# A gMLP input weight fetched from DRAM product by product in layer two instead of being held in SBUF

## The chip, the cores and the metric

The kernel runs on one core of a Trainium2 chip. The core has five engines that work side by side and meet at semaphores: PE (TensorE, matmuls), ACT (ScalarE), DVE (VectorE), POOL (GpSimd) and SP (SyncE, which here only issues transfers). Each engine takes its own instructions strictly in the order of the program. Data sits in DRAM, in SBUF (128 partitions) and, for the results of matmuls, in the banks of PSUM. The metric is the device time of one execution in microseconds; before the change the median of three runs is 1395.2 (1394.91 to 1395.57).

## The reference

Two layers, each a linear attention block and then a gMLP, both with a layernorm ahead of them and a residual connection, on 2048 tokens of width 512 in float32, 896 gated features:

```python
def _A_ref(x, wqkv, wo):                    # linear attention, 32 heads of 16
    pq, pk = phi(q), phi(k)
    kv = einsum("bhsd,bhse->bhde", pk, v); z = einsum("bhsd->bhd", pk)
    o = (pq @ kv) / (pq . z + 1e-6)
    return o @ wo
def _B_ref(x, w_in, w_sp, b_sp, w_out):     # gMLP
    z = _gelu(x @ w_in)                     # 2 * 896 features
    z1 = z[..., :Fh]
    z2 = _layernorm(z[..., Fh:], axis=-1)
    g = einsum("ts,bsf->btf", w_sp, z2) + b_sp[None, :, None]
    return (z1 * g) @ w_out
x = A_x
x = x + _A_ref(_layernorm(x), A_wqkv, A_wo)
x = x + _B_ref(_layernorm(x), B_w_in, B_w_sp, B_b_sp, B_w_out)
x = x + _A_ref(_layernorm(x), A_wqkv, A_wo)
x = x + _B_ref(_layernorm(x), B_w_in, B_w_sp, B_b_sp, B_w_out)
```

Both layers use the same weights. The change concerns the first half of `w_in`, 512 x 896, from which `z1` is made.

## The kernel before

**Numbers.** Every float32 operand of a matmul is held as two parts of type float32r: a high part, rounded by ACT (`high`, L100), and a low part, source minus high part, made by DVE (`low`, L103) or by POOL (L109). A product of two such operands is three matmuls (`mm3`, L113): high by high, high by low, low by high. The third is the first to need the low part of the first operand.

**Room.** SBUF is cut into slots: 22 pages of 128 x 512 floats (`pages`), 6 quads of four pages (`quads`), 4 bigs of seven pages (`bigs`); PSUM into 8 banks. `Slots.get` gives the slot that has been free longest, `put` appends it to the free list; whoever first writes a slot waits by semaphore for the last user of its former tile. The order of all instructions on every engine is the order of the Python program.

**Stages of a layer.** `P1` (q, k, v side of the attention), `transition`, `P2` (attention's output, residual, layernorm, both halves of the gMLP's input product), `P4` (spatial product, gate, output product). The change is in `P2`.

**P2's steps.** There are 16 token tiles of 128 rows. Step s of `P2.run` (L684) works on several tiles at once, in this order of the program: loads for the next steps on SP (`loadx`, `qturn.load`); `b_high`, `b_low`: the turned and divided queries of tile s in two parts; `c`: 12 matmuls, attention's output of tile s-1; `c2`, `c_stats`: residual and statistics (DVE, then three small instructions on POOL, `rs` L182 and L183 and `nb` L185); `c3`: store of x on SP, normalisation on ACT (L191), turn; `a` for a later tile (POOL L544); `d_high`, `d_low`: the turned normalised rows of tile s-2 in two parts (from step 6 on through DRAM, `yt`); `e4`: normalisation of an earlier gate row; `e`, `e2`, `e3`: 24 matmuls of 448 columns for the second half of `w_in`, gelu, statistics (POOL again, `rs` and `nb`); then `f` twice.

**The products `f`.** The first half of `w_in` is used turned: product (n, f) takes 128 features f and 512 tokens n, 12 matmuls of 512 columns, gelu on ACT (L677), store to DRAM (L680). There are 7 x 4 = 28 products in a layer, seven for each group of four tiles. The first group is complete in step 5, so the products run from step 6 on, two per step (one in steps 9, 13, 17); step 18 runs two, and the five that are left run at the head of `P4.run` (L1002), so that the last seven stand back to back.

**The weight before.** `w_in1()` (L167) makes a `Weight` of seven pieces of one page. `fetch` loads a piece into a page (SP), `piece` splits it into the parts `h` and `l` in two bigs (ACT L101, POOL L109 where `pool` is true) and gives the page back. The transition fetches two pieces; steps 1 to 7 of `P2.run` split one each, last thing in the step. Each layer does it anew; the bigs are given back at the head of `P4.run`.

**POOL's other work in P2.** In layer one `sums.tick()` (from step 8 on) makes sums of spatial weights on POOL (L772) from pages that SP loads just before; in layer two nothing of that is left.

Of the kernel before, what the change touches and what calls it, by code (L numbers as in the profile page):

```python
# [53 lines left out]
def mixer_kernel(ctx: ExitStack, tc: tile.TileContext, x_in, wqkv, wo_d, win1_d, win2_d, wsp_d, bsp_d, wout_d,  # L54
# [63 lines left out]

    class Weight:


        def __init__(self, slots, shape, pieces, turned=False):
            self.slots, self.shape, self.pieces, self.turned = slots, shape, pieces, turned
            self.h = self.l = None
            self.raw = deque()
            self.n_load = self.n_split = 0
# [6 lines left out]
        def piece(self, pool=False):  # L133
            if self.n_split >= len(self.pieces):
                return False
            if self.h is None:
                self.h = self.slots.get(self.shape, F32R)
                self.l = self.slots.get(self.shape, F32R)
            if not self.raw:
                self.fetch()  # L140
            r = self.raw.popleft()
            n = len(self.shape)
            flat = "p a b -> p (a b)" if n == 3 else "p a b c -> p (a b c)"
            s = slice(self.n_split * 512, (self.n_split + 1) * 512)
            h, l = self.h.rearrange(flat)[:, s], self.l.rearrange(flat)[:, s]
            if self.turned:
                split(feats(h, True), feats(l, True), feats(r, False), pool)
            else:
                split(h, l, r, pool)
            pages.put(r)  # L150
            self.n_split += 1
            return True
# [7 lines left out]

    def w_square(src, off, turned=False):
# [5 lines left out]
    def w_in1():  # L167
        return Weight(bigs, [P, NF, 4, P], [win1_d[f] for f in range(NF)])
# [78 lines left out]
    class P1:  # L247
# [164 lines left out]
        def run(self):  # L412
# [5 lines left out]
            for s in range(1, NT + 2):  # L418
                self.loadx(s + 3)
                self.turn.load(s + 1)  # L420
                turned = 2 <= s < NT and s not in self.turn.by_pe
# [35 lines left out]
    def transition(p1, p2):  # L457
# [21 lines left out]
        p2.win1.fetch()  # L479
        p2.win1.fetch()  # L480
# [44 lines left out]
    class P2:  # L525
        def __init__(self, p1):
            self.L = L = p1.L
            self.p1 = p1
            self.win1, self.win2 = w_in1(), p1.win2
# [135 lines left out]
        def f(self):  # L665
# [4 lines left out]
            w = self.win1  # L670
            b = banks.get(PAGE)
            for c in range(4):
                mm3(b, (w.h[:, f, c, :], w.l[:, f, c, :]), (h[:, c, :], l[:, c, :]), c == 0, c == 3)
# [10 lines left out]
        def run(self, sums):  # L684
            w1 = self.win1
            for s in range(1, NT + 3):
                self.loadx(s + 1)
                self.qturn.load(s + 1)
                if s in self.qturn.by_pe:
# [48 lines left out]
                w1.piece(True)  # L738
                w1.fetch()
# [55 lines left out]
    class P4:  # L795
# [203 lines left out]
        def run(self, nxt):  # L999
# [3 lines left out]
            while p2.f():  # L1003
                pass
            p2.win1.free()
# [100 lines left out]
```

## Time and profile before

| | |
|---|---|
| median of the runs | 1395.2 us |
| the profiled execution's own time | 1395.31 us |
| its span, first instruction to last | 1393.5 us |
| granted TensorE clock | 1.00 |
| matmuls | 6270 |
| DRAM read, written | 156.63 MB, 67.90 MB |
| P2's products in layer one, layer two | from 189.2 us, from 879.3 us |

How to read what follows. Times are in us from the start of the span, unless ns is written. A row of a timeline gives start, duration, engine, line of the kernel, operation, tile written, arrow, tiles read; in brackets the idle time before and who ended it. Tiles are named by their slots: `pg` a page, `qd` a quad, `bg` a big, `bank` a PSUM bank. `SPq` is SP issuing a transfer. A row of groups gives the count, total busy time, mean ns of one, and idle time before. Matmuls of 512 columns are listed with 0.39 us but start every 0.23 us, since they overlap. A row of transfers gives the kilobytes of one and the median us from issue to landing.

### The profile page before, as it was taken

Reading aid. Unit: us, or ns where it says so; the run is one execution under the profiler, and the core shown is the slowest. Engines: PE = TensorE matmul, PEld = TensorE weight load, DVE = VectorE, ACT = ScalarE, POOL = GpSimd, SP = SyncE. Lnnn points to the kernel's source line nnn. Section 1 sums busy time; section 2 is a strip of 40 time slices with the busy share of each in tenths; the row PEclk is TensorE's granted clock in tenths of the full one; section 3 lists DMA queues with packets and bytes.
Section 4 is the critical chain, followed back from the end, with each engine's and each line's share of the span. In section 5 each row is a group of like instructions: output and inputs, shape, how many; then the busy total and the mean of one; then the engine's idle time right before and its main releaser. Section 6 shows DMA issues by size and latency. Waiting matters only on the chain.

```text
span 1393.5 us, 17586 instructions
## 1 busy us (share of the span) xinstructions
PE 1387.4 (100%) x6270; PEld 1164.0 (84%) x6270; DVE 879.5 (63%) x1251; ACT 582.1 (42%) x899; POOL 416.9 (30%) x502
## 2 busy tenths in 40 slices
PE   9999999999999999999999999999999999999998
PEld 7888888888888888888888888888888888888887
DVE  6775777853755587664567767876426445776642
ACT  6674543444432234241366655444333432342410
POOL 3343344543135541431023424432100000223310
PEclk9999999999999999999999999999999999999999
DMA  5542256776679964354645314555334323544542
GB/s 176 168 131 59 90 166 218 259 226 217 215 235 295 298 228 136 121 203 159 211 129 176 111 46 121 174 176 175 104 122 142 101 96 129 168 134 156 169 143 91
DMA packets 142457, 225.70 MB, mean 162 GB/s; under 512 B 11937, under 2 KB 50593, under 8 KB 142369
## 3 DMA queue, kind: packets, MB, share of 16 engines
q1 hardware_dynamic: 142368, 224.57, 50.1%
q8 instruction: 49, 0.80, 0.3%
q14 instruction: 40, 0.32, 0.1%
HBM read 156.63 MB, written 67.90 MB: 161 GB/s over the span
## 4 chain that ended last, share of the span: by engine, by line
PE 98%; DVE 1%; DMA 0%; POOL 0%; ACT 0%; issue 0%; SPq 0%; POOLq 0%; ACTq 0%
PE bank L117 19%; PE bank L116 19%; PE bank L115 19%; PE bank L897 13%; PE bank L898 13%; PE bank L899 13%; PE bank L203 1%; PE bank L390 0%; DMA pg<-in_wsp_dram 0%; POOL pg L772 0%; ACT z_z L191 0%; DVE st L178 0%; ACT qd L101 0%; POOL rs L183 0%; DVE den L557 0%
## 5 line engine op out<-in xcount | busy, mean ns | idle before, releaser
L898 PE MATMUL bank<-qd,pg 128*128 128x512 f32 x800 | 311.4, 389 | 0.0
L897 PE MATMUL bank<-qd,pg 128*128 128x512 f32 x800 | 311.4, 389 | 0.0
L899 PE MATMUL bank<-qd,pg 128*128 128x512 f32 x800 | 311.4, 389 | 0.0
L863 DVE TENSOR_TENSOR qd<-qd,qd 128x1024 fp32r<-128x1024 f32 x112 | 157.9, 1410 | 157.2 <-ACT qd L856 154.2
L856 ACT ACTIVATE qd<-qd 128x1024 fp32r<-128x1024 f32 x112 | 118.6, 1059 | 239.1 <-DMA qd<-s 101.7
L899 PEld LDWEIGHTS bank<-qd,pg 128*128 128x128 f32 x800 | 150.2, 188 | 31.4
L897 PEld LDWEIGHTS bank<-qd,pg 128*128 128x128 f32 x800 | 150.1, 188 | 31.2
L898 PEld LDWEIGHTS bank<-qd,pg 128*128 128x128 f32 x800 | 150.2, 188 | 31.0
L919 POOL TENSOR_TENSOR bg<-bg,pg 128x512 f32<-128x512 f32 x56 | 78.9, 1413 | 320.7 <-DMA pg<-z 308.6
L117 PE MATMUL bank<-qd,pg 128*128 128x512 f32 x384 | 149.9, 390 | 0.0
L182 POOL TENSOR_SCALAR rs<-mv 128x1 f32<-128x1 f32 x96 | 38.0, 396 | 355.4 <-DVE mv L180 351.8
L191 ACT ACTIVATE pg<-pg,nb,rs 128x512 f32<-128x512 f32 x63 | 51.0, 810 | 179.0 <-POOL nb L185 172.8
L772 POOL TENSOR_TENSOR pg<-pg,pg 128x512 f32<-128x512 f32 x64 | 93.9, 1467 | 94.4 <-DMA pg<-in_wsp_dram 88.5
L115 PE MATMUL bank<-qd,pg 128*128 128x512 f32 x288 | 112.3, 390 | 0.0
L116 PE MATMUL bank<-qd,pg 128*128 128x512 f32 x288 | 112.3, 390 | 0.0
L115 PE MATMUL bank<-bg,qd 128*128 128x448 f32 x256 | 94.1, 368 | 0.0
L117 PE MATMUL bank<-bg,qd 128*128 128x448 f32 x256 | 93.6, 366 | 0.1
L116 PE MATMUL bank<-bg,qd 128*128 128x448 f32 x256 | 93.7, 366 | 0.0
L117 PE MATMUL bank<-qd,bg 128*128 128x512 f32 x224 | 87.5, 391 | 0.0
L116 PE MATMUL bank<-qd,bg 128*128 128x512 f32 x224 | 87.5, 390 | 0.0
L115 PE MATMUL bank<-qd,bg 128*128 128x512 f32 x224 | 87.3, 390 | 0.0
L116 PE MATMUL bank<-wo,qd 128*128 128x512 f32 x224 | 87.2, 389 | 0.0
(128 smaller groups left out, 2606.9 us busy)
## 6 DMA issues: line engine op xcount, KB each, us to landing
qd<-s SPq DMA_DIRECT2D x64, 512.0 KB, 3.5
qd<-in_wsp_dram SPq DMA_DIRECT2D x48, 512.0 KB, 4.2
pg<-in_wsp_dram SPq DMA_DIRECT2D x64, 256.0 KB, 5.2
s<-pg SPq DMA_DIRECT2D x64, 256.0 KB, 5.0
pg<-x SPq DMA_DIRECT2D x64, 256.0 KB, 3.1
z<-pg SPq DMA_DIRECT2D x56, 256.0 KB, 2.7
pg<-z SPq DMA_DIRECT2D x56, 256.0 KB, 3.9
x<-pg SPq DMA_DIRECT2D x48, 256.0 KB, 2.6
```

The lines of the kernel that those rows point to most:

```text
L115: nc.tensor.matmul(out, ah, bh, start=start, stop=False)
L116: nc.tensor.matmul(out, ah, bl, start=False, stop=False)
L117: nc.tensor.matmul(out, al, bh, start=False, stop=stop)
L182: nc.gpsimd.tensor_scalar(rs, mv[:, 1:2], LN_EPS, None, op0=OP.add)
L191: nc.scalar.activation(y, x, AF.Identity, bias=nb, scale=rs)
L772: nc.gpsimd.tensor_tensor(t, a, b, op=OP.add)
L856: nc.scalar.activation(w[:, 0], r, AF.Copy)
L863: nc.vector.tensor_sub(w[:, 1], r, w[:, 0].bitcast(F32))
L897: m(out, h[:, o], w[:, 0, j, :], start=start, stop=False, skip_group_check=True)
L898: m(out, h[:, o], w[:, 1, j, :], start=False, stop=False, skip_group_check=True)
L899: m(out, l[:, o], w[:, 0, j, :], start=False, stop=stop, skip_group_check=True)
L919: nc.gpsimd.tensor_tensor(u, u, z1, op=OP.mult)
```

## The change

In layer one each split of a piece of the weight also notes its two parts for storing; at the head of every step of `P1.run` and `P2.run`, `flush` issues up to four of the noted stores on SP. The stores go to 14 DRAM tiles of a page each. In layer two the weight takes no bigs and nothing is split. `Parts` keeps up to three products' parts ahead, each in two pages (high, low) that POOL's transfers fill from those DRAM tiles; product (n, f) takes the next two pages and gives them back as soon as its matmuls are in the program. The parts are fetched anew for each of the four groups, 28 x 2 transfers of 256 KB. `fetch` stands at the end of each step from step 4 on, and behind each product at the head of `P4.run`. The transfer's source is declared float32 and its destination float32r.

```diff
--- before.py
+++ after.py
@@ -116,11 +116,18 @@
         nc.tensor.matmul(out, ah, bl, start=False, stop=False)
         nc.tensor.matmul(out, al, bh, start=False, stop=stop)
 
+    stores = deque()
+
+    def flush(n=4):
+        for _ in range(min(n, len(stores))):
+            d, part = stores.popleft()
+            nc.sync.dma_start(d, part.bitcast(F32))
+
     class Weight:
 
 
-        def __init__(self, slots, shape, pieces, turned=False):
-            self.slots, self.shape, self.pieces, self.turned = slots, shape, pieces, turned
+        def __init__(self, slots, shape, pieces, turned=False, keep=None):
+            self.slots, self.shape, self.pieces, self.turned, self.keep = slots, shape, pieces, turned, keep
             self.h = self.l = None
             self.raw = deque()
             self.n_load = self.n_split = 0
@@ -148,6 +155,8 @@
             else:
                 split(h, l, r, pool)
             pages.put(r)
+            if self.keep is not None:
+                stores.extend(zip(self.keep[self.n_split], (h, l)))
             self.n_split += 1
             return True
 
@@ -158,6 +167,28 @@
         def free(self):
             self.slots.put(self.h, self.l)
 
+    class Parts:
+
+
+        def __init__(self, kept, times, ahead):
+            self.todo = deque(kept * times)
+            self.ahead = ahead
+            self.have = deque()
+
+        def fetch(self):
+            while self.todo and len(self.have) < self.ahead:
+                parts = [pages.get([P, 4, P], F32R) for _ in range(2)]
+                for t, d in zip(parts, self.todo.popleft()):
+                    nc.gpsimd.dma_start(t, d.rearrange("p (c f) -> p c f", c=4))
+                self.have.append(parts)
+
+        def take(self):
+            if not self.have:
+                self.fetch()
+            return self.have.popleft()
+
+    kept_in1 = [[dram.tile(PAGE, F32, name=f"win1_{f}_{i}") for i in range(2)] for f in range(NF)]
+
     def w_square(src, off, turned=False):
         return Weight(quads, [P, 4, 512], [src[c * P:(c + 1) * P, off:off + 512] for c in range(4)], turned)
 
@@ -165,7 +196,7 @@
         return Weight(bigs, [P, 4, 512], [wo_d[c * P:(c + 1) * P, :] for c in range(4)])
 
     def w_in1():
-        return Weight(bigs, [P, NF, 4, P], [win1_d[f] for f in range(NF)])
+        return Weight(bigs, [P, NF, 4, P], [win1_d[f] for f in range(NF)], keep=kept_in1)
 
     def w_in2():
         return Weight(bigs, [P, 4, FH], [win2_d[f] for f in range(NF)])
@@ -418,6 +449,7 @@
             for s in range(1, NT + 2):
                 self.loadx(s + 3)
                 self.turn.load(s + 1)
+                flush()
                 turned = 2 <= s < NT and s not in self.turn.by_pe
                 if turned:
                     self.T_high(s)
@@ -476,8 +508,9 @@
         banks.put(zb)
         p2.a(0)
         p1.late_phi()
-        p2.win1.fetch()
-        p2.win1.fetch()
+        if p2.L == 0:
+            p2.win1.fetch()
+            p2.win1.fetch()
         p2.zeps = small.tile([P, 32], F32, name="zeps", bufs=1)
         nc.vector.tensor_reduce(p2.zeps, p2.zbc.rearrange("p (h d) -> p h d", d=16), axis=mybir.AxisListType.X,
                                 op=OP.add)
@@ -526,7 +559,7 @@
         def __init__(self, p1):
             self.L = L = p1.L
             self.p1 = p1
-            self.win1, self.win2 = w_in1(), p1.win2
+            self.win1, self.win2 = (w_in1() if self.L == 0 else Parts(kept_in1, NCHK, 3)), p1.win2
             self.qturn, self.xturn = Turn(f"qt{L}", range(5), True), Turn(f"yt{L}", range(4))
             self.qp, self.qT, self.x, self.ms, self.xB, self.z, self.zms = {}, {}, {}, {}, {}, {}, {}
             self.fq = deque()
@@ -668,9 +701,15 @@
             n, f = self.fq.popleft()
             h, l = self.xT[n]
             w = self.win1
+            if self.L == 0:
+                wh, wl = w.h[:, f], w.l[:, f]
+            else:
+                wh, wl = w.take()
             b = banks.get(PAGE)
             for c in range(4):
-                mm3(b, (w.h[:, f, c, :], w.l[:, f, c, :]), (h[:, c, :], l[:, c, :]), c == 0, c == 3)
+                mm3(b, (wh[:, c, :], wl[:, c, :]), (h[:, c, :], l[:, c, :]), c == 0, c == 3)
+            if self.L > 0:
+                pages.put(wh, wl)
             if f == NF - 1:
                 quads.put(*self.xT.pop(n))
             t = pages.get(PAGE)
@@ -686,6 +725,7 @@
             for s in range(1, NT + 3):
                 self.loadx(s + 1)
                 self.qturn.load(s + 1)
+                flush()
                 if s in self.qturn.by_pe:
                     self.c(s - 1)
                     self.b_high(s)
@@ -735,8 +775,11 @@
                 self.f()
                 self.fq.extend(self.fnext)
                 self.fnext = []
-                w1.piece(True)
-                w1.fetch()
+                if self.L == 0:
+                    w1.piece(True)
+                    w1.fetch()
+                elif s >= 4:
+                    w1.fetch()
                 if s > 7:
                     sums.tick()
                 if s >= NT + 1:
@@ -1001,8 +1044,10 @@
             self.prepare(0, 0)
             self.fetch(2)
             while p2.f():
-                pass
-            p2.win1.free()
+                if p2.L > 0:
+                    p2.win1.fetch()
+            if p2.L == 0:
+                p2.win1.free()
             self.prepare(1, 1)
             self.fetch(3)
             self.prepare(None, 2)
```

## The prediction

> **What bounds the kernel now.** I read the page first (busy shares, then the chain that ended last), then the windows of the stage in which layer two would use the new transfers, then the timeline of each engine inside it.
>
> ```profile
> span 1393.5 us, 17586 instructions
> PE 1387.4 (100%) x6270; PEld 1164.0 (84%) x6270; DVE 879.5 (63%) x1251; ACT 582.1 (42%) x899; POOL 416.9 (30%) x502
> PE 98%; DVE 1%; DMA 0%; POOL 0%; ACT 0%; issue 0%; SPq 0%; POOLq 0%; ACTq 0%
> ```
>
> TensorE is busy for all but 6 us of the span and is 98% of the chain. The change adds and removes no matmul, so its gain can be no more than a few stalls that are hardly there; the question is whether it makes PE wait. The same stage (from the first gMLP product to the first of the last seven) in layers one and two:
>
> ```profile
> core 0: us, PE busy (x) PEld busy (x) DVE busy (x) ACT busy (x) POOL busy (x), PEclk, DMA share, GB/s
> 189.20:332.70 143.50, 143.44 (x662) 123.82 (x661) 96.25 (x152) 57.75 (x94) 65.82 (x101) 1.00 0.69 222
> 879.30:1022.40 143.10, 143.10 (x662) 124.01 (x662) 88.12 (x152) 58.42 (x94) 39.97 (x81) 1.00 0.49 155
> ```
>
> Layer one carries the spatial sums on POOL besides: 26 us more POOL work and 67 GB/s more traffic cost 0.4 us in 143. So traffic alone is cheap here: the change's 56 loads of 256 KB (14.7 MB) in some 160 us are about 90 GB/s, which takes layer two to about 245 GB/s, just above layer one. What the 0.4 us is shows in the chain of waits, and it is the pattern to fear:
>
> ```profile
> 222.66 5.49 DMA pg<-in_wsp_dram
> 229.68 1.29 POOL pg L772
> 232.03 0.28 POOL nb L185
> 233.70 0.70 DVE qd L104
> 234.44 0.48 PE bank L117
> ```
>
> POOL executes in order. While it waits at L772, the row statistics behind it wait too; ACT normalises late, the split of the turned row (`d_low`) is late, and PE's third matmul of `e` stands still. In layer two POOL will stand in issues of transfers instead.
>
> **Layer one: the 14 stores.** Step s issues on SP the two stores of piece s-1. A store must wait for POOL's subtract, and the whole SP queue waits with it:
>
> ```profile
> 189.92 1.29 POOL L109 TENSOR_TENSOR bg<-pg,bg 128x512 fp32r<-128x512 f32 x1
> ...
> 190.93 0.38 SPq L97 DMA_DIRECT2D pg<-qt  x1
> 194.36 0.38 SPq L227 DMA_DIRECT2D qt<-pg  x1
> ```
>
> Step 6 shows it: the subtract ends at 191.21, SP is done with its loads at 191.31 and has nothing until 194.36. Two issues of 0.38 us end at 192.1. Cost 0, covered by 3.0 us of SP idleness; without that cover it would be 0.8 us of SP per step, not on PE's path.
>
> **Layer two, removed.** Seven loads on SP, seven roundings on ACT (0.6 us each), seven subtracts on POOL. PE waits for none of them, but the subtract stands in POOL's order and slows a small DVE add beside it. Rows of the timelines of POOL, DVE, ACT and PE in order of time (start and duration in us, then the instruction, in brackets how long the engine had been idle and for whom):
>
> ```profile
> 861.86 1.29 POOL L109 TENSOR_TENSOR bg<-pg,bg 128x512 fp32r<-128x512 f32 x1
> 862.37 0.18 DVE L180 BATCH_NORM_AGGREGATE mv<-st 128x2 f32<-128x6 f32 x1
> 863.25 0.22 POOL L182 TENSOR_SCALAR rs<-mv 128x1 f32<-128x1 f32 x1
> 863.76 0.19 DVE L557 TENSOR_TENSOR den<-den,zeps 128x32 f32<-128x32 f32 x1
> 869.32 0.26 POOL L185 TENSOR_SCALAR nb<-mv,rs 128x1 f32<-128x1 f32 x1
> 869.55 1.28 POOL L109 TENSOR_TENSOR bg<-pg,bg 128x512 fp32r<-128x512 f32 x1
> 873.44 0.56 POOL L182 TENSOR_SCALAR rs<-mv 128x1 f32<-128x1 f32 x1 [2.61 <-DVE mv L180]
> 875.05 0.82 ACT L191 ACTIVATE pg<-pg,nb,rs 128x512 f32<-128x512 f32 x1 [4.65 <-POOL nb L185]
> 880.30 1.12 DVE L557 TENSOR_TENSOR den<-den,zeps 128x32 f32<-128x32 f32 x1
> 886.32 0.62 ACT L101 ACTIVATE qd<-pg 128x512 fp32r<-128x512 f32 x1
> 886.97 0.69 DVE L104 TENSOR_TENSOR qd<-pg,qd 128x512 fp32r<-128x512 f32 x1 [1.51 <-ACT qd L101]
> 887.93 0.36 PE L117 MATMUL bank<-bg,qd 128*128 128x448 f32 x1
> 890.92 0.26 POOL L185 TENSOR_SCALAR nb<-mv,rs 128x1 f32<-128x1 f32 x1
> ```
>
> Two savings follow. The statistic at 863.25 was ready at 862.55 and stood behind the subtract; step 4 of POOL moves up by some 0.6 us. The add L557 takes 1.12 us beside a subtract and 0.19 alone: 0.93 us per step.
>
> **Layer two, added: the issues on POOL.** What does one cost there? The trace has no transfer issued by POOL. From below stands SP's 0.38 us, from above POOL's slowest operation on a page, L917's 1964 ns:
>
> ```profile
> L109 POOL TENSOR_TENSOR bg<-pg,bg 128x512 fp32r<-128x512 f32 x14 | 18.1, 1292 | 8.7 <-ACT bg L101 8.7
> L917 POOL TENSOR_TENSOR bg<-bg 128x512 f32<-128x512 f32 x12 | 23.6, 1964 | 56.8 <-DVE bg L950 56.8
> pg<-in_wsp_dram SPq DMA_DIRECT2D x64, 256.0 KB, 5.2
> z<-pg SPq DMA_DIRECT2D x56, 256.0 KB, 2.7
> pg<-in_win_dram SPq DMA_DIRECT2D x28, 256.0 KB, 3.0
> ```
>
> I take d = 1.2 us, near POOL's ordinary page operation (1.29), since there it is the same engine that works through the 128 rows. Landing after the issue's end: 3.0 - 0.4 = 2.6 us, as the same weight's loads do now; the other end is 5.2 - 0.4 = 4.8. The fetch asks for three products at step 4 (six issues), none at step 5, then what was used (four, or two where one product ran). Three places can reach PE.
>
> *Place 1, the six issues of step 4.* They start behind the `nb` of `e3`, at 869.58 - 0.6 = 868.98, and end at 868.98 + 6 x 1.2 = 876.18. Queued behind them is the `rs` of step 5 (873.44 before): 2.74 us late. ACT L191 waits for it, everything on ACT and DVE up to step 6 follows rigidly; 0.93 comes back at 880.30, so `d_low` in step 6 is 1.81 us late. Before, it ended at 887.66 and PE wanted it at 887.93: slack 0.27. PE stalls 1.81 - 0.27 = 1.54 us.
>
> *Place 2, the fourth product, in step 7.* It is fetched after step 6, behind the `nb` that ended at 891.18, now 1.81 later: 892.99. Two issues and the landing: 892.99 + 2.4 + 2.6 = 897.99. PE's third matmul of it, which needs the low part, is the row of 895.59 below, shifted by the 1.54: 897.13. Stall 0.86 us.
>
> ```profile
> 895.59 0.39 PE L117 MATMUL bank<-qd,bg 128*128 128x512 f32 x1
> ...
> 1031.02 0.39 PE L117 MATMUL bank<-qd,bg 128*128 128x512 f32 x1
> ...
> 1033.74 0.39 PE L117 MATMUL bank<-qd,bg 128*128 128x512 f32 x1
> ...
> 1025.63 0.26 POOL L185 TENSOR_SCALAR nb<-mv,rs 128x1 f32<-128x1 f32 x1
> ...
> 1029.04 1.65 SPq L819 DMA_DIRECT2D qd<-in_wsp_dram  x2
> ```
>
> *Between.* From step 8 on the fetched product is not wanted before the step after next, over 10 us later, and ACT and DVE gain on PE: 0.
>
> *Place 3, the last seven products.* They run back to back, 2.72 us each (1031.02 to 1033.74). Three are there; four are fetched behind the `nb` that ends at 1025.89. The low parts land at 1025.89 + 2.4k + 2.6 = 1030.9, 1033.3, 1035.7, 1038.1 against PE at 1031.02, 1033.74, 1036.46, 1039.18: just in time. The two spatial loads of 512 KB at 1029.04 collide with the second; I charge 0.4 us.
>
> The Trainium skill, page "DMA: Bandwidth & Descriptors", section "Latency and other measured facts", puts the first byte of a GpSimd-issued transfer at about 1 us and of SP's at about 0.6. Read as an issue of 1.0 us (an estimate from that page), the three places give 0.34, 0.46 and 0.4, and a time of 1396.5; no row here can decide.
>
> Sum: 1.54 + 0.86 + 0.4 = 2.8 us on this execution's 1395.31 (span 1393.5 and 1.8 around it; 0.1 above the runs' median of 1395.2): 1398.1.
>
> **Pages.** Six of the 22 are now held by parts. Counted through the code's order of gets and puts, 10 to 15 were free in these steps; now it is 4 to 12, so a page comes back within a step. The tightest: `b_low` of a step takes the page of the step before's first gated output.
>
> ```profile
> 889.33 2.15 SPq L680 DMA_DIRECT2D z<-pg  x2
> 892.79 0.63 DVE L104 TENSOR_TENSOR pg<-pg,pg 128x512 fp32r<-128x512 f32 x1
> ```
>
> Its store lands at 889.33 + 2.7 = 892.03, wanted 0.76 later. Cost 0; with a landing of 5.2 us DVE would be 1.7 late there, in the step where the fourth product is late anyway.
>
> **The rivals.**
>
> *Hidden.* If an issue takes no more than 0.94 us (868.98 + 6d - 873.44 = 0.93 + 0.27), place 1 vanishes, place 2 shrinks to 0.1 and place 3 is its 0.4: 1395.3 to 1395.8, not slower. For it: SP's 0.38, and POOL's idleness. Against it: POOL works in software through its pages in 1.3 us.
>
> *POOL as the bound.* Issues of 1.97 us (L917). Place 1: 868.98 + 11.82 - 873.44 - 0.93 - 0.27 = 6.2; place 2: 891.18 + 6.43 + 3.94 + 2.6 - 895.59 - 6.16 = 2.4; the tail, where 3.94 us of issues per product run against 2.72 of PE, 1025.89 + 15.76 + 2.6 - 1039.18 = 5.1. Sum 13.7: 1409. For it: the rounded destination type may need more than a plain copy, and DVE and POOL do disturb one another (0.19 to 1.12). Against: no row shows such a slow simple step. The skill's page "SBUF — State Buffer", section "Who interferes with whom", would give it a cause: GpSimd cannot write descriptors while DVE is in a two-port mode. DVE's rows of these steps show no copy or scalar form that the page lists, so the trace speaks against that here.
>
> *Parts land late.* With 4.8 us after the issue: place 2 grows to 3.06, the tail to 1025.89 + 2.4 + 4.8 - 1031.02 = 2.1; sum 6.7: 1402. For it: the two queues share the engines when both are at work. Against: layer one at 222 GB/s.
>
> *Faster.* Only through stalls that PE has now in layer two; with PE busy 143.10 of 143.10 there are none to take. 1394.9 at best.
>
> **Chances.** Forecast (an issue of 0.95 to 1.5 us, 1396.3 to 1401.5) 0.40; hidden 0.31; POOL as the bound 0.16; late parts 0.10; faster 0.03. A measurement of this kernel tells apart about 0.2%, 2.8 us. Slower by more than that: a good half of the forecast's case with both bad rivals, 0.50; within it 0.47; faster 0.03. The range holds the bound's case with what a product between places 2 and 3 might add to it: 1394.9 to 1411.
>
> **What would show it.** Right: on POOL six issues in a row after step 4 and an `rs` behind them later than DVE's `mv`; a gap on PE of 1 to 2 us in the `e` of step 7; one at the fourth product's third matmul; small ones among the last seven. Hidden: POOL's `rs` still waits for DVE's `mv` everywhere. Bound: POOL solid from step 4 to step 9 and a gap before each of the last four products. Wrong in kind: a gap in layer one, a wait of SP or DVE for a page, or matmuls of the product itself at another pace than 0.23 us.

## The result and the profile after

| | before | after |
|---|---|---|
| median of 20 runs each | 1394.97 us | 1396.98 us |
| lowest, highest | 1394.12, 1395.69 | 1396.05, 1401.25 |
| ratio, 95% interval | | 1.0015 (1.0009 to 1.0022) |
| profiled execution: time, span | 1395.31, 1393.5 | 1397.45, 1395.2 |

The changed kernel is 2.0 us, 0.15%, slower. That is under the 0.2% within which the prediction calls two kernels the same, and 20 runs of each are just enough to put the interval above 1.

The first rows of its page: the busy shares, the chain that ended last, and two rows of its transfer table.

```profile
span 1395.2 us, 17747 instructions
...
PE 1388.1 (99%) x6270; PEld 1163.3 (83%) x6270; DVE 878.3 (63%) x1251; ACT 578.7 (41%) x892; POOL 438.7 (31%) x551
...
PE 92%; DMA 2%; DVE 2%; ACT 1%; POOL 1%; issue 1%; SPq 0%; POOLq 0%; ACTq 0%; DVEq 0%
...
pg<-in_wsp_dram SPq DMA_DIRECT2D x64, 256.0 KB, 5.2
...
pg<-win POOLq DMA_DIRECT2D x56, 256.0 KB, 6.0
```

PE has the same 6270 matmuls in the same order, so the two traces can be laid side by side matmul by matmul: start of the k-th matmul after, less its start before. A difference that stays put means that PE runs at its old pace; each jump is a stall. The table further down does that for every run. For the change it has four jumps: -0.20 us in the first 72 us, +0.39 at the `e` near 234 in layer one, +0.74 at 895, +0.45 near 1037; nothing else moves by more than 0.01. The first two also come and go in the runs further down whose code there is the same as the change's (-0.96 to +0.02, and -0.48 to +0.39), so they are the spread of single executions. What the change makes is 0.74 + 0.45 = 1.19 us of stalls in layer two.

The first of them, in the timelines of PE and POOL of the changed kernel (start, duration, instruction; in brackets the idle time before and who ended it):

```profile
889.44 2.24 POOL L182 DMA_DIRECT2D pg<-win  x4
...
895.09 0.39 PE L117 MATMUL bank<-qd,pg 128*128 128x512 f32 x1
895.83 0.47 PE L115 MATMUL bank<-qd,pg 128*128 128x512 f32 x1 [0.35 <-ACT pg L222]
896.14 0.40 PE L116 MATMUL bank<-qd,pg 128*128 128x512 f32 x1
896.37 0.49 PE L117 MATMUL bank<-qd,pg 128*128 128x512 f32 x1
```

Matmuls follow each other in 0.23 us; here 0.74 us pass between 895.09 and 895.83, which is 0.51 too much, and the rest of the stall is lost in wider steps over the next few matmuls. This is the fourth product, step 7's second. Its high part was issued from 889.44 to 890.09 and landed at 895.70, its low part at 896.32, just before the first and the third matmul. The bracket names an activation that ended at nearly the same moment; the same row of the run without conversion, further down, names the transfer instead, and the stall is gone in every run that asks for the part earlier.

Why did a transfer take 5.6 us after its issue had ended? The table of windows of the two kernels around it (busy us and count of each engine, granted clock, busy share of the 16 DMA engines, GB/s), after and then before:

```profile
888.00:890.00 2.00, 2.00 (x12) 1.85 (x11) 1.93 (x5) 0.73 (x2) 1.55 (x4) 1.00 0.84 243
890.00:892.00 2.00, 2.00 (x12) 1.85 (x11) 1.28 (x3) 0.00 (x0) 1.68 (x4) 1.00 0.99 264
892.00:894.00 2.00, 2.00 (x11) 1.69 (x10) 1.93 (x5) 0.00 (x0) 0.56 (x1) 1.00 1.05 326
894.00:896.00 2.00, 1.65 (x8) 1.10 (x7) 0.84 (x1) 1.01 (x2) 1.88 (x3) 1.00 1.21 382
```

```profile
888.00:890.00 2.00, 2.00 (x12) 1.85 (x11) 1.97 (x5) 2.00 (x5) 0.05 (x1) 1.00 0.28 55
890.00:892.00 2.00, 2.00 (x12) 1.85 (x11) 1.97 (x3) 0.95 (x2) 1.82 (x4) 1.00 0.67 247
892.00:894.00 2.00, 2.00 (x10) 1.68 (x9) 1.97 (x4) 0.00 (x0) 0.44 (x1) 1.00 0.85 286
894.00:896.00 2.00, 2.00 (x10) 1.68 (x9) 1.93 (x5) 0.00 (x0) 0.87 (x2) 1.00 0.34 124
```

Before, the transfer engines are busy for a share of 0.28 to 0.85; after, they are full from 890 to 896 (shares over 1 are full). Nine transfers of 256 KB (a load of the turned array, two stores of z, the loads of x and of the queries, four parts) are issued between 887.2 and 891.7 and come in one behind the other, the last six 0.4 to 0.9 us apart. The views of single transfers agree: here the load of x took 5.7 us to land and that of the queries 6.0, where the kernel before has 3.1 and 3.4 for the same two.

The second stall, in the timeline of PE, is the sixth of the last seven products:

```profile
1036.93 0.39 PE L115 MATMUL bank<-qd,pg 128*128 128x512 f32 x1
1037.15 0.39 PE L116 MATMUL bank<-qd,pg 128*128 128x512 f32 x1
1037.70 0.50 PE L117 MATMUL bank<-qd,pg 128*128 128x512 f32 x1 [0.15 <-DMA pg<-win]
```

It waits for the low part, issued at 1029.77 and landed 7.9 us later, while the two spatial loads of 512 KB are under way.

Two more pieces lie outside PE's work. From PE's last matmul to the end of the span the kernel before takes 3.77 us, the changed one 4.11. Both have the last store landing 2.77 us after that matmul; then SP goes through further waits on the semaphores of the transfers, 0.06 us each, eight of them where there were three (0.27 us in the trace), and POOL's clearing of the semaphores and what follows takes 0.07 us more. So 0.34 us is the bill for POOL's transfers at the end of the program. And time less span is 2.2 us where it was 1.8: 0.43 us. In sum 1.19 + 0.34 + 0.43 = 1.96 us, against the 2.01 between the medians. The stalls are those of one execution, and executions differ: the 20 runs of the change reach from 1396.05 to 1401.25 us.

### The profile page after: what moved, and what is told of

The parts are those of the page before. It is cut to its first block, busy times and chain, and to the rows that moved or that the text cites. A ratio compares the mean times of both kernels' runs of the same rounds, so it can differ in the third digit from the quotient of the medians.

```text
span 1395.2 us, 17747 instructions
## 1 busy us (share of the span) xinstructions
PE 1388.1 (99%) x6270; PEld 1163.3 (83%) x6270; DVE 878.3 (63%) x1251; ACT 578.7 (41%) x892; POOL 438.7 (31%) x551
## 3 DMA queue, kind: packets, MB, share of 16 engines
q0 software_dynamic: 8064, 14.68, 3.8%
## 4 chain that ended last, share of the span: by engine, by line
PE 92%; DMA 2%; DVE 2%; ACT 1%; POOL 1%; issue 1%; SPq 0%; POOLq 0%; ACTq 0%; DVEq 0%
PE bank L117 18%; PE bank L115 17%; PE bank L116 17%; PE bank L942 13%; PE bank L941 13%; PE bank L940 13%; DMA pg<-win 1%; DVE st L209 1%; PE bank L234 0%; DMA win<-bg 0%; DMA pg<-in_wsp_dram 0%; PE bank L421 0%; POOL rs L214 0%; DMA yt<-pg 0%; POOL pg L182 0%
## 5 line engine op out<-in xcount | busy, mean ns | idle before, releaser
L940 PE MATMUL bank<-qd,pg 128*128 128x512 f32 x800 | 311.2, 389 | 0.0
L941 PE MATMUL bank<-qd,pg 128*128 128x512 f32 x800 | 311.2, 389 | 0.0
L942 PE MATMUL bank<-qd,pg 128*128 128x512 f32 x800 | 311.2, 389 | 0.0
L899 ACT ACTIVATE qd<-qd 128x1024 fp32r<-128x1024 f32 x112 | 118.7, 1060 | 239.8 <-DMA qd<-s 98.5
L117 PE MATMUL bank<-qd,pg 128*128 128x512 f32 x496 | 193.8, 391 | 0.2 <-DMA pg<-win 0.2
L941 PEld LDWEIGHTS bank<-qd,pg 128*128 128x128 f32 x800 | 150.2, 188 | 31.3
L940 PEld LDWEIGHTS bank<-qd,pg 128*128 128x128 f32 x800 | 150.2, 188 | 31.2
L942 PEld LDWEIGHTS bank<-qd,pg 128*128 128x128 f32 x800 | 150.2, 188 | 30.9
L115 PE MATMUL bank<-qd,pg 128*128 128x512 f32 x400 | 156.1, 390 | 0.3 <-ACT pg L222 0.3
L116 PE MATMUL bank<-qd,pg 128*128 128x512 f32 x400 | 155.9, 390 | 0.0
L117 PEld LDWEIGHTS bank<-qd,pg 128*128 128x128 f32 x496 | 93.1, 188 | 20.9 <-DVE pg L104 0.8
L115 PEld LDWEIGHTS bank<-qd,pg 128*128 128x128 f32 x400 | 75.1, 188 | 16.0 <-ACT pg L222 0.7
L116 PEld LDWEIGHTS bank<-qd,pg 128*128 128x128 f32 x400 | 75.1, 188 | 15.6 <-DVE qd L104 0.3
```

The source lines that it names most:

```text
L115: nc.tensor.matmul(out, ah, bh, start=start, stop=False)
L116: nc.tensor.matmul(out, ah, bl, start=False, stop=False)
L117: nc.tensor.matmul(out, al, bh, start=False, stop=stop)
L899: nc.scalar.activation(w[:, 0], r, AF.Copy)
L940: m(out, h[:, o], w[:, 0, j, :], start=start, stop=False, skip_group_check=True)
L941: m(out, h[:, o], w[:, 1, j, :], start=False, stop=False, skip_group_check=True)
```

## The experiments

Each is run beside the kernel before on the same chip, where that kernel's median was 1394.74 to 1394.89. Columns: median, ratio with interval; then from the profiled execution, laid beside that of the kernel before, how far PE falls back in layer two up to 893 us, from 893 to 1000, and from 1000 to 1060 (the last seven products); from PE's last matmul to the span's end; and time less span (median over the runs). All in us. Stalls differ from execution to execution: the eight runs of e1 reach from 1396.11 to 1400.38.

| run | median | ratio (95%) | to 893 | to 1000 | to 1060 | end | outside |
|---|---|---|---|---|---|---|---|
| the change | 1396.98 | 1.0015 (1.0009 to 1.0022) | 0.00 | 0.74 | 0.45 | 4.11 | 2.2 |
| e1 four ahead | 1398.89 | 1.0028 (1.0018 to 1.0038) | 0.00 | 3.44 | 0.00 | 4.11 | 1.8 |
| e2 before, mask by POOL | 1394.80 | 1.0001 (0.9992 to 1.0009) | 0.09 | 0.01 | 0.00 | 3.82 | 1.8 |
| e3 no conversion | 1396.89 | 1.0015 (1.0006 to 1.0024) | 0.00 | 1.14 | 0.00 | 4.09 | 2.2 |
| e4 issued by SP | 1401.52 | 1.0046 (1.0033 to 1.0059) | 0.00 | 0.00 | 6.79 | 3.71 | 1.9 |
| e5 halves | 1404.11 | 1.0065 (1.0052 to 1.0077) | 1.21 | 1.72 | 5.67 | 4.10 | 1.8 |
| e6 stores only | 1394.71 | 0.9999 (0.9990 to 1.0008) | 0.00 | 0.00 | 0.00 | 3.58 | 1.8 |
| e7 before, sums early | 1394.72 | 0.9998 (0.9989 to 1.0007) | -0.01 | -0.01 | 0.00 | 3.76 | 1.8 |
| e9 four, three, four ahead | 1396.55 | 1.0014 (1.0005 to 1.0022) | 0.00 | 0.59 | 0.00 | 4.38 | 1.8 |
| e11 four ahead in a ring | 1395.65 | 1.0005 (0.9996 to 1.0014) | 0.00 | 0.00 | 0.00 | 4.11 | 2.1 |
| e12 ring, sums early | 1395.00 | 1.0004 (0.9995 to 1.0013) | 0.00 | 0.00 | 0.00 | 4.10 | 2.2 |
| e13 ring, issued by SP | 1395.70 | 1.0008 (0.9999 to 1.0016) | 0.00 | 0.00 | 0.88 | 3.71 | 1.8 |

**Four products ahead.**

```diff
-Parts(kept_in1, NCHK, 3)
+Parts(kept_in1, NCHK, 4)
```

> Edit: layer two keeps up to four products fetched ahead instead of three; nothing else. My theory now: the two stalls of PE inside layer two, 0.74 us at the fourth product's third matmul (895.1) and 0.45 us at the sixth of the last seven (1036.5), come from parts that land some 5.5 us after their issue. Asked for one product earlier, both go: the PE difference matmul by matmul loses about 1.2 us and the span falls from 1395.2 to about 1394.0. What lies outside the span stays at about 2.2 us, so the time is 1396.2, about 0.1% above the kernel before. Rival, place 1 of the prediction: eight issues in step 4 instead of six hold POOL 8 x 0.57 = 4.6 us from 869.5 to 874.1, past the 873.0 at which step 5's rs was computed, and the stall moves to the e of step 7, up to 0.9 us. Rival, contention: the stalls come from the traffic whatever the order of the transfers, and stay at 0.7 and 0.4 us.

Both stalls go, as the theory said, and yet the kernel is 1.9 us slower than the change: there are two new stalls of 1.12 and 2.32 us, at the `e` of steps 8 and 10. Neither rival has it: POOL's issues in step 4 end at 873.57 and cost PE nothing. The timelines of DVE, ACT and PE of this run show what does:

```profile
893.71 1.09 DVE L273 STREAM_TRANSPOSE pg<-pg 128x512 f32<-128x512 f32 x1 [4.31 <-DMA z<-pg]
900.40 0.61 ACT L101 ACTIVATE qd<-pg 128x512 fp32r<-128x512 f32 x1
901.07 0.47 PE L115 MATMUL bank<-bg,qd 128*128 128x448 f32 x1 [0.54 <-ACT qd L101]
919.44 1.10 DVE L273 STREAM_TRANSPOSE pg<-pg 128x512 f32<-128x512 f32 x1 [2.69 <-DMA z<-pg]
926.79 0.47 PE L115 MATMUL bank<-bg,qd 128*128 128x448 f32 x1 [1.76 <-ACT qd L101]
```

DVE's transpose at 893.71 stood 4.31 us until a store of z had landed: the transpose writes a page, and the next free page was the one that this store was still reading. Eight pages held leave too few. The same wait, in a smaller form, is in the change itself. Groups of DVE's `b_low` (busy us, mean ns, idle us before them and whose release ended it), before and after:

```profile
L104 DVE TENSOR_TENSOR pg<-pg,pg 128x512 fp32r<-128x512 f32 x71 | 53.2, 750 | 12.2 <-ACT pg L101 11.7
```

```profile
L104 DVE TENSOR_TENSOR pg<-pg,pg 128x512 fp32r<-128x512 f32 x71 | 53.4, 753 | 17.7 <-DMA z<-pg 11.7 <-ACT pg L101 5.5
```

In the change DVE stands 11.7 us in all for stores that still read a page, where the row of before names none: its wait for ACT shrank by 6.2 us, and 5.5 us of idleness are new. PE did not feel it there.

**Four ahead in a ring.** The parts land in the two bigs of 14 KB per partition that the weight held before, seven slots in turn; the pages are left alone.

```diff
...
-                parts = [pages.get([P, 4, P], F32R) for _ in range(2)]
+                parts = [t[:, self.k % NF] for t in (self.h, self.l)]
+                self.k += 1
...
-            if self.L > 0:
-                pages.put(wh, wl)
...
```

> Edit: four products fetched ahead as in e1, same issues at the same places on POOL, but the parts land in the two large buffers (14 KB per partition each) that the weight held before, used as a ring of seven slots, and not in pages. What it tells: where e1's two new stalls of PE (0.9 to 1.1 us at 900.6, 2.3 us at 924) come from. My theory, pages: eight pages held leave too few for DVE, whose transpose at 893.71 waited 4.31 us for a page that a store of z still held; with no page held by the parts both stalls go, and so do places 2 and 3: PE within 0.4 us of the kernel before at the end of the weight's work, span about 1393.8, time 1395.6 to 1396.0. Rival, traffic: the page was late because the z store and the loads beside it shared the engines with the eight transfers; then the store lands as late as before and, with DVE no longer waiting for a page, at least the wait for the x load at 921.53 and its 2.3 us stall stay: about 1398.

All four stalls are gone: from 330 us to the end PE does not leave its old pace by 0.01 us. The traffic is the same and the transfers land little sooner than in the change, where the median was 6.0 us (first the row of the transfer table: KB each, median us from issue to landing; then the `b_low` group of this run):

```profile
bg<-win POOLq DMA_DIRECT2D x56, 256.0 KB, 5.2
```

```profile
L104 DVE TENSOR_TENSOR pg<-pg,pg 128x512 fp32r<-128x512 f32 x71 | 53.3, 751 | 12.4 <-ACT pg L101 12.0
```

The step-7 group is as crowded as before: its four parts took 6.2 to 6.5 us here, against 6.2 to 6.5 in the change. So late landing costs PE only where the part is asked for too late, and e1's stalls were pages. What is left, 1395.65 against 1394.89, is little more than the 0.34 us at the end and 0.3 outside the span, and its interval includes 1.

**Four, three, four.** Four products asked for at step 4 and among the last seven, three between.

```diff
...
-                    w1.fetch()
+                    w1.fetch(4 if s == 4 else None)
...
-                    p2.win1.fetch()
+                    p2.win1.fetch(4)
```

> Edit: four products are asked for at step 4 and, after the steps, among the last seven; three in the steps between, as in the change. Parts stay in pages. Theory: the fourth product is there early (place 2, 0.74 us, goes), the sixth of the last seven too (place 3, 0.45 us, goes), and the pages suffice, since no more than six are held from step 7 on: the span falls by about 1.2 us against the change, to 1394.0; with 1.8 to 2.2 us outside it 1395.8 to 1396.2. Rival: the first stall of e1 (900.6) was made by the eight pages held up to step 6, and stays here at 0.9 us: 1396.7 to 1397.1.

The theory is half right. Both old stalls and e1's are gone, but one of 0.59 us appears one step later: at 908.23 the sixth product waits for a part issued at 903.17 and landed at 908.10. The stall at 895 had not been covering it: in the change the same part is issued at 900.76 and lands at 906.18, 2.9 us before PE starts the sixth product at 909.11. POOL is 2.4 us later here. Its statistics at 889.30 are 1.0 us behind those of the change (888.26), and then DVE's `b_low` in step 7 stands 2.14 us for a store of z, where it stood 0.71 in the change; the statistics on POOL and the issues behind them move with it (the change's row, then this run's):

```profile
891.04 0.69 DVE L104 TENSOR_TENSOR pg<-pg,pg 128x512 fp32r<-128x512 f32 x1 [0.71 <-DMA z<-pg]
893.43 0.69 DVE L104 TENSOR_TENSOR pg<-pg,pg 128x512 fp32r<-128x512 f32 x1 [2.14 <-DMA z<-pg]
```

So most of the lateness is again a wait for a page, although only six are held from step 7 on. Of the first 1.0 us some 0.5 come from the two more issues in step 4, behind which `rs` of step 5 starts at 873.57 and not at 873.03.

**No conversion.** The parts are moved as float32 in both places.

```diff
-nc.gpsimd.dma_start(t, ...)
+nc.gpsimd.dma_start(t.bitcast(F32), ...)
```

> Edit: the 56 loads of layer two write the page through a view of type float32, so that POOL's transfers do not turn float32 into the rounded type. Theory A, the transfers land late because both queues share the engines: issue 0.57 us and landing 6.0 us unchanged, stalls of 0.74 and 0.45 us unchanged, 1397.0. Theory B, the conversion is what makes them slow: landing falls to about 3 us after the issue, as SP's plain loads of the same size had in the kernel before, and both stalls go: about 1395.8.

The time is the change's. POOL's queue counts 4480 packets where it counted 8064, and the median landing is 5.4 us where it was 6.0, but e1 and e9 convert and have 5.3 and 4.9. The crowded group of step 7 is no faster, and the stall there is 1.14 us; the one among the last seven is absent, since its part landed at 1035.89 and not at 1037.65. The row of the stall names the cause that the change's row hid:

```profile
896.21 0.47 PE L115 MATMUL bank<-qd,pg 128*128 128x512 f32 x1 [0.79 <-DMA pg<-win]
```

**Issued by SP.** The same transfers at the same places of the program, on SP's queue and, as in e3, without the conversion.

```diff
-nc.gpsimd.dma_start(t, ...)
+nc.sync.dma_start(t.bitcast(F32), ...)
```

> Edit: the same 56 loads at the same places of the program, but issued by SP and without a change of type. Theory A, sharing: they still collide with x, qt and the spatial loads; behind SP's other issues of the step they start no earlier, so the stalls stay within some 0.5 us of 1.2, but the 0.43 us outside the span goes if a POOL queue costs it: 1396.0 to 1396.5. Theory B, POOL's queue is the slow one: landing 3 us, no stalls, no cost outside the span: 1395.0, the kernel before. A risk for both: six issues of 0.38 us in a row on SP, and their waits for pages, hold up SP's loads and stores behind them.

Neither theory holds: the kernel is 4.5 us slower than the change. The median landing is 4.3 us and nothing is late in the steps, where SP asks for the fourth product at 887.27, 2.2 us sooner than POOL did; but the last seven products lose 6.79 us. SP's timeline and PE's:

```profile
1028.56 1.87 SPq L182 DMA_DIRECT2D pg<-win  x4
1030.48 0.94 SPq L862 DMA_DIRECT2D qd<-in_wsp_dram  x2
1031.51 0.42 SPq L719 DMA_DIRECT2D z<-pg  x1
1031.98 1.32 SPq L182 DMA_DIRECT2D pg<-win  x2
...
1040.62 0.76 PE L115 MATMUL bank<-qd,pg 128*128 128x512 f32 x1 [3.13 <-DMA pg<-win]
```

SP is in order too, and between the parts stand the stores of z, each of which waits for the gelu of a product. So the sixth product's high part is issued at 1031.98, behind the two spatial loads of 512 KB, and lands 8.5 us later. In the change POOL, which has nothing else to do there, issues all eight parts in one go and reaches this one at 1029.25:

```profile
1027.06 4.34 POOL L182 DMA_DIRECT2D pg<-win  x8 [0.17 <-issue]
```

A transfer does not land sooner from POOL's queue (those eight take 3.8 to 9.4 us); it is issued sooner. Beside the 3.13 us PE has a first stall of 1.38 at 1031.63, and the rest are matmuls at a slower pace: behind the 3.13 us the next seven start some 0.43 us apart in place of 0.23, and the granted clock is 0.50 from 1042 to 1044.

**Ring, issued by SP.** As e11, on SP's queue.

> Edit: as e11 (four products ahead, parts in the ring that holds no pages), but issued by SP without a change of type. What it tells: whether POOL's queue has a price when nothing comes too late. Theory: yes, 0.27 us at the end of the span, where SP waits one after the other for four more semaphores (those of POOL's transfers), 0.07 us on POOL behind that; here the time from PE's last matmul to the end is 3.7 to 3.8 us again instead of 4.1. PE as in the kernel before, if the parts come early enough; 1394.9 to 1395.3. Rival: SP's queue is the limit; among the last seven products its issues stand behind the two spatial loads of 512 KB and wait for their buffers, and with four in hand one still comes late, by up to 3 us: 1396 to 1398.

The end is back to 3.71 us and time less span to 1.8, so the 0.34 us belongs to POOL's transfers; with it e4 (3.71) agrees. But the rival is right about PE: among the last seven one part is still late behind the spatial loads, 0.88 us, and the sum, 1395.70, is that of e11.

**Halves.** Each part in two transfers of 128 KB.

```diff
-                    nc.gpsimd.dma_start(t, d.rearrange("p (c f) -> p c f", c=4))
+                    r = d.rearrange("p (c f) -> p c f", c=4)
+                    for k in (0, 2):
+                        nc.gpsimd.dma_start(t[:, k:k + 2, :], r[:, k:k + 2, :])
```

> Edit: each part comes in two transfers of 128 KB in place of one of 256 KB, so that POOL issues 112 instead of 56. Theory of place 1 (issues that keep POOL from step 5's rs reach PE in the e of step 7), if an issue costs by the transfer, 0.57 us each: twelve issues from 869.5 hold POOL 6.8 us to 876.3, rs (before at 873.44) is 2.9 us late, and with the 0.93 and the 0.27 us of slack of the prediction PE stalls about 1.7 us in step 7's e; the fourth product lands 2.2 us later too. Sum 1399 to 1400. Rival, an issue costs by the row or byte it moves: twelve halves take the 3.45 us of the six whole ones, and the time stays at 1397.

An issue does not cost by its bytes. POOL's rows in step 4, this run's and then the change's, and the `e` of step 7 in this run:

```profile
869.17 6.62 POOL L184 DMA_DIRECT2D pg<-win  x12 [0.22 <-issue]
875.86 0.23 POOL L215 TENSOR_SCALAR rs<-mv 128x1 f32<-128x1 f32 x1
...
887.17 0.39 PE L117 MATMUL bank<-qd,pg 128*128 128x512 f32 x1
888.10 0.47 PE L115 MATMUL bank<-bg,qd 128*128 128x448 f32 x1 [0.54 <-ACT qd L101]
888.40 0.36 PE L116 MATMUL bank<-bg,qd 128*128 128x448 f32 x1
888.82 0.47 PE L117 MATMUL bank<-bg,qd 128*128 128x448 f32 x1
```

```profile
869.51 3.45 POOL L182 DMA_DIRECT2D pg<-win  x6 [0.22 <-issue]
873.03 0.23 POOL L213 TENSOR_SCALAR rs<-mv 128x1 f32<-128x1 f32 x1
```

Twelve half transfers take 6.62 us, six whole ones 3.45: 0.55 and 0.57 each. A half has the same 128 rows, so a cost by the row is not excluded. Now `rs` is at 875.86, 2.42 us after its 873.44 in the kernel before, and PE stalls in step 7's `e` by 1.21. The prediction's rule for this place, lateness less 0.93 and less 0.27, gives 1.22, or 1.35 with the 0.13 us by which PE was ahead of the kernel before when it came there. The fourth product is later too (most of the 1.72 up to 1000 us), and the tail loses 5.67: there POOL issues twelve in a row and then stands 2.66, 0.91 and 0.53 us for its own earlier transfers before it issues the next. So the 1404.1 lies above the 1399 to 1400 that was expected.

**Stores only.** Layer one stores the parts as in the change, layer two loads, splits and holds as before.

```diff
-(w_in1() if self.L == 0 else Parts(kept_in1, NCHK, 3))
+w_in1(self.L == 0)
...
```

> Edit: layer one stores the parts as in the change, layer two loads, splits and holds the weight as the kernel before. What it tells: whether the 14 stores cost anything, in layer one or outside the span. Theory of the prediction: 0, the time is the kernel before's, 1394.9, and PE's difference to it stays under 0.2 us through layer one. Rival: the change's larger stall at 234 (0.3 us instead of 0.2) or its 0.43 us outside the span belong to the stores: 1395.2 to 1395.4.

1394.71 against 1394.74: the stores cost nothing, neither in layer one (0.47 us less than the profiled run of before at the `e` near 234) nor outside the span.

**One transfer by POOL in the kernel before.**

```diff
-nc.sync.dma_start(mask, mask_d)
+nc.gpsimd.dma_start(mask, mask_d)
```

> Edit: the kernel before, with one change: the mask of 128 rows is loaded at the start by a transfer issued by POOL instead of SP, so that the program has one transfer on POOL's queue. Theory A: that a POOL queue is in use at all adds about 0.43 us outside the span (time less span 1.8 to 2.2 us): time 1395.4, span 1393.5 as before. Theory B: the 0.43 us belongs to the 56 transfers or to the stores at the end of layer one, or is the spread between chips: time less span stays at 1.8, time 1395.0 as the kernel before beside it.

Theory B holds. A queue on POOL by itself adds nothing outside the span, and 0.05 us at its end. Nor do the 56 transfers explain the 0.43: e1, e5 and e9 have them all and are at 1.8, while the change, e3, e11 and e12 are at 2.1 to 2.2, each within 0.15 over its runs. It goes with the compiled program; by what, no run here shows.

**Sums early.** Layer one's first spatial load asked for at the end of step 7, in the kernel before, and in the ring.

```diff
+                if s == 7 and self.L == 0:
+                    sums.fetch()
```

> Edit: the kernel before, with layer one's first spatial-sum load asked for one step earlier (at the end of step 7), so that POOL does not wait for it at its first sum. Theory: POOL's wait at 229.68 and with it PE's stall of 0.2 to 0.3 us at 234 go: 1394.6 beside 1394.8, hardly more than the spread. Rival: the pages it takes early, or the loads beside the others in step 7, cost as much again: 1394.8 to 1395.2.

> Edit: as e11, and layer one's first spatial-sum load asked for at the end of step 7, as in e7. What it tells: whether the best form of the change reaches the kernel before. Theory: PE gains the 0.45 us that e7 gained at 234, and keeps the 0.3 us at the end of the span and what lies outside: 1395.1 to 1395.4, not below the kernel before and not below e7. Rival: what lies outside the span is 1.8 us in this program, as in e1, e5 and e9: 1394.8, level with the kernel before.

Not settled, and too small to be. PE's stall at 234 is gone in both (-0.47 and -0.45 us against the profiled run of before), but e6 and e13, whose layer one is not so edited, show as much (-0.47 and -0.48). The medians, 1394.72 against 1394.89 and 1395.00 against 1394.74, include 1 in their intervals. No form of the change came out below the kernel before; its best, with ring and early sums, is level with it.

## Why the prediction was right, and where it was not

The time of 1398.1 was 1.1 us too high, and the measured 1396.98 lies in its range. The steps held less well than their sum, and that the sum came so near is in part luck: 1.54 us did not come at all, and 0.77 us came that the prediction had not reckoned with. The time lies where the forecast's case was priced (1396.3 to 1401.5), but that case's condition, an issue of 0.95 to 1.5 us, was not met.

**PE bounds, nothing to gain.** Right. In the runs without stalls PE keeps its pace in layer two to 0.01 us; the loads, roundings and subtracts that were removed gave nothing.

**The stores.** Cost 0, right: e6.

**The savings on POOL and DVE.** The add of DVE after the reduction takes 0.19 us in step 7 of the change; that was right. POOL in step 4 moved up by 0.3 us, not by 0.6 (its issues start at 869.51, where 868.98 was forecast).

**Place 1, 1.54 us: the step that failed.** The chain from POOL's issues through `rs`, the normalisation and `d_low` to PE is there, and its slack of 0.93 + 0.27 was right to some 0.1 us: e5 shows it. The issue was mis-sized. d = 1.2 us was taken from POOL's operations on a page; it is 0.57, nearer to SP's 0.38, and the halves show that it does not go with the bytes. At 0.57 the six issues end at 872.96, before 873.44, and place 1 is 0, as the rival *hidden* had it for any d up to 0.94. The `rs` does stand behind the issues, as forecast: DVE's `mv` was done at 872.00, `rs` starts at 873.03, still sooner than before. (That rival's 0.1 for place 2 leaves out the 0.27 us of lateness that a d of 0.94 makes; with it place 2 is 0.34.)

**The landing: failed the other way.** 2.6 us after the end of the issue was assumed, 4.8 as the far end; the part that PE waited for took 5.6 us. The premise behind it, that traffic alone is cheap since layer one bears 222 GB/s, compared means over 143 us. Bursts decide: the transfer engines are full for 6 us around step 7, though the mean of the changed kernel over this stage (first row; the kernel before in the second) is 0.77 and 227 GB/s, close to layer one and to the 245 that the prediction reckoned.

```profile
879.30:1024.00 144.70, 144.35 (x666) 124.54 (x666) 85.55 (x151) 57.56 (x93) 59.36 (x119) 1.00 0.77 227
```

```profile
879.30:1024.00 144.70, 144.70 (x669) 125.31 (x669) 88.86 (x154) 58.96 (x95) 39.97 (x81) 1.00 0.48 153
```

So the pattern was that of *parts land late*, whose price of 1402 came out too high mainly because it kept the issue of 1.2 us. With 0.57 in it, place 1 is gone and the other two are 1.5 and 0.8, which makes 1397.7.

**Place 2, 0.86 us.** Right in place; that its size of 0.74 is near is luck, since its errors nearly cancel. The issues began at 889.44 and not at 892.99, 3.6 us sooner; the first two took 1.2 us in place of 2.4; the low part landed 5.7 us after the end of its issue and not 2.6; and PE, without the stall of place 1, wanted it 1.35 us sooner than forecast. The first matmul waited too, for the high part, and not only the third for the low one.

**Between, 0.** Right: in the change the sixth product's two parts land 2.9 and 1.7 us before PE wants them. The margin is not large, as the 0.59 us in e9 show, where POOL was 2.4 us later.

**Place 3, 0.4 us.** It was 0.45, with the two spatial loads beside it, though the late product is the sixth of the last seven where the fifth was named. The 0.4 was a charge that the prediction did not work out, so its size is luck.

**Pages, cost 0.** Right for PE, but closer than the count of 4 to 12 free pages suggested. `b_low` did wait 0.71 us for a store in step 7 and 11.7 us in all, which is DVE's wait for a page that the prediction had named as a sign of being wrong in kind; with two pages more held it is 3.44 us on PE. The prediction took 2.7 us, the median, for the store's landing; in the kernel before, the store issued at 889.33 took 4.09. A count of free slots says nothing of whether the last user of the next one is done.

**Not foreseen.** 0.34 us of semaphore waits at the end, 0.43 outside the span: 0.77 of the 2.0 us.

The Trainium skill's page "DMA: Bandwidth & Descriptors", section "Latency and other measured facts", was read for an issue of 1.0 us, and the sum by it was 1396.5; the page gives a time to the first byte and no issue time, and the issue was 0.57 us, so that sum's nearness is luck too. No row here shows a first byte. The page's pair of figures, about 1 us and about 0.6, can only be set beside landings in step 4 of the change, where the engines are still free: SP's load of the queries landed 2.68 us after its start and POOL's first part 3.20.

## What to carry to other kernels

Price a transfer by the moment at which it is issued: add up what is asked for within a few microseconds around it, and not the mean rate of the stage. Whether it stalls anyone is then a matter of when it is asked for, and the room for asking earlier should come from buffers that nobody else is cycling through: in the pages the fourth product ahead cost 3.4 us, in the freed bigs nothing. And a part asked for earlier holds its buffer longer: look at who waits for that buffer, and at what is issued behind that wait, as in the run with four, three and four products ahead.

## What the runs showed of the hardware

- POOL is busy 0.57 us with issuing a transfer of 128 rows of 2 KB and 0.55 us with one of half the bytes; SP's issue of the same takes some 0.5 us where it does four in a row (1.87 us).
- On POOL's queue, turning float32 into float32r on the way takes 8064 packets instead of 4480 for the same 14.68 MB; the kernel's time is the same with and without (1396.98 and 1396.89).
- Neither queue lands a transfer sooner when the engines are full (up to 9.4 us from POOL's queue, 8.6 from SP's). What a queue of its own gave was an issue that stood behind nothing: the sixth of the last seven products was asked for 2.7 us sooner, and PE lost 0.45 us over these seven in place of 6.79.
- A longer wait costs PE more than itself: behind waits of 3.13 us (e4) and 3.23 us (e5) the next seven matmuls start some 0.43 us apart in place of 0.23, in e4 at a granted clock of 0.50. Behind the 1.38 us in e4 PE is back at 0.23 after four.
- The program's end is not free of the queues in use: with the 56 transfers on POOL's queue, SP goes through five more waits of 0.06 us after the last store has landed.
- Time less span keeps to within 0.15 us in all runs of one compiled program and lies between 1.8 and 2.2 us from program to program: 0.4 us between two kernels need not come from anything in their traces.
